# Attention into a gated FFN: a planner that knows four matmul forms, other weight and load times, and wider score steps for the fourth batch

## The chip, the cores and the metric

The kernel runs on one core of a Trainium2 chip. The metric is device time in microseconds (us) of one execution. The engines are TensorE (PE in the profile; PEld is its weight load), VectorE (DVE), ScalarE (ACT), GpSimd (POOL) and SyncE (SP), which here only issues DMAs. The clock granted to TensorE was 1.000 of full speed in the profiled execution.

## What is computed

There are 8 batches (B), 8 heads (H) and 576 rows (S) of 64 values (D). Each head sees 16 beacon keys in front of its 576 keys; the beacons are always visible, the others causally.

```
scores = q @ concat(beacon_k, k).T / sqrt(64)      # causal over k, beacons free
a      = softmax(scores)
x      = a @ concat(beacon_v, v)                   # -> 4608 rows of 512 (heads side by side)
out    = (relu(x @ w_gate) * (x @ w_val)) @ w_out  # 512 -> 1536 -> 512
```

Inputs and output are float32; the kernel multiplies in bf16 and sums in float32.

## The kernel before

**Attention.** For a batch, each of q and k comes in by pairs of heads (`load_pair`, and `load_half` for batch 0) and a rest (`load_rest`: the "K" and "Q" loads), v in five blocks (`load_v`). A load goes by SP into one of eight staging tiles `st`, is rounded to bf16 by POOL (batch 0: POOL or DVE; line 514, v line 467), turned by four products with the identity (line 525) and copied out by ACT or DVE into `kT` and `qT`. The order inside a batch is "K Q 0 0 1 1 v v 2 2 3 3 v v v v", numbered from 0.

`quad` computes the scores of two pairs of heads (a group; two groups per batch) in steps. A step (`quad_scores`, line 743) is a run of 64x64 products into PSUM banks. Each score tile then goes through `softmax`: the minimum with the mask on DVE (line 691), the exponential on ACT (line 698), the reciprocal on DVE (line 704), the scaling on POOL (line 709). `STEPS` takes few banks in a step, `STEPS2` four; which of them a batch uses is set by BIGSTEP. `last` computes the last 16 rows of all heads (line 793, 128x32 products).

`finish` turns the probabilities: on PE for batch 0 and the last rows of batches 0 and 1 (line 819), otherwise by a transposing DMA on SP (line 829, `pTb<-pb`). Then come the values: AB and CDE for each pair (line 839, 128x64 products) and F for the last rows (line 862, 128x128 products). They are copied into `xT`, the FFN's input.

**FFN.** `ffn` works on spans of rows: 240 and 336 (batch 0), then 512 each, at the end 448. For each of 12 blocks of 128 hidden columns it makes four gate products (line 900) and four value products (line 905); ACT takes the relu (line 911), DVE multiplies (line 916). Then the output products (line 931) follow, DVE or ACT copies out (lines 465 and 463), and SP stores. The weights come by nine DMAs that POOL issues and that cast on the way (line 477): gate and value for hidden columns 0, 512 and 1024, then three pieces of the output weights.

**The order.** Nothing is ordered by the program's text. Each piece of work is a `Task` with an engine, a modelled cost, dependencies, buffers it holds, and a priority; `Plan.order` simulates the engines and writes out one fixed order for each. It takes, over all engines, the task that can begin first; among equals the one with the smaller `late`, then the smaller priority number. For PE `late` is worked out from `part`, the form of the products: -1 for a task of the small form that runs now, and 1 for a task of another form that has waited less than its `lazy` time (LAZY, 20 us, for values of batches from 2 on; LAZY1, 0, for batch 1). A change of form is modelled as 0.1 us (SWITCH). Before, form 1 stands for the last rows' scores and all values (AB, CDE and F), form 2 for the score steps, form 0 for the rest.

When PE has a planned gap before 160 us, the plan puts in filler products (line 990) that compute nothing. Weights may be issued from W0 on, one in W_STEP; the score steps of batch b and group g from PACE x (b + g/2); batch 0's two parts (AB, CDE) from the times in AFTER. HELD and BEHIND name loads (batch, number) that wait: HELD until a weight piece has been issued, BEHIND until the probabilities of a group (batch, group) are scaled. The wait holds for all later loads of that batch too. It is a tiny POOL memset (line 535), on which the loads depend.

PSUM has eight banks: seven are shared from the start (at most 5 for scores, 3 for the FFN, 3 for values and turns); the eighth is the fillers' and joins at 36 us of the plan's time.

Of the kernel before, what the change touches and what calls it, by code (L numbers as in the profile page):

```python
# [17 lines left out]


BACKLOG = 4.0  # L20
RANK1 = -10.0
AHEAD = 2.0
WWORK = -15.0
FILLED = 160.0
# [5 lines left out]
LAGS = {"PE": 0.22, "ACT": 0.16, "DVE": 0.14, "POOL": 0.1, "DMA": 0.1}  # L30
LAZY = 20.0
LAZY1 = 0.0
ON_PE = 2
BIGSTEP = 3
PEQ = lambda b, g: b < 1
ENG = [("POOL", "DVE"), ("POOL",), ("POOL",)]
F_MOST = 3
HELD = {(1, 3): ('v', 0, 0), (1, 5): ('g', 0, 512), (1, 11): ('o', 0, 0)}
BEHIND = {(2, 7): (1, 1)}
MARK = 0.08  # L40
AB_FIRST = 0
W_FIRST = 0
# [4 lines left out]
ORDER0 = ("k00", "q00", "K", "Q", "k10", "q10", "v", "v", "k01", "q01", "k11", "q11", "v", "v", "v")  # L47
W_COLS = [(0, 512), (512, 512), (1024, 512)]
W_ROWS = 4
W0 = 16.5  # L50
W_STEP = 3.4
W_ISSUE = 0.85
W_MOVE = 0.72
V_MOVE = 1.25
# [3 lines left out]
FIRST_SPANS = [240, 336]  # L58
LAST_SPAN = 448
FIRST_MOST = 3  # L60
AFTER = [[0.0, 8.0]]
PACE = 39.0


class Slots:
# [104 lines left out]
class Plan:  # L170
# [7 lines left out]
    def add(self, engines, cost, run, deps=(), holds=(), prio=0.0, lag=None, part=0, lazy=0.0, after=0.0, move=0.0):  # L178
        t = Task(engines if isinstance(engines, tuple) else (engines,), cost, run, deps, holds, prio, lag, part, lazy, move)
        t.ready = after  # L180
        for d in t.deps:
            d.users.append(t)
        self.tasks.append(t)
        return t

    def order(self):
# [11 lines left out]
        part = 0  # L198
# [23 lines left out]
        while True:  # L222
            best = None
            for e in queue:
                for t in queue[e]:
                    times = begin(t, e)
                    if times is None:
                        continue
                    at, could = times
                    late = 0  # L230
                    if e == "PE":
                        late = -1 if part and t.part == part else 1 if part != t.part and at < t.ready + t.lazy else 0
                    key = (at, late, t.prio)
                    if best is None or key < best[0]:
                        best = (key, t, e)
            if best is None:
                break
            (at, _, _), t, e = best
            for x in t.engines:
                queue[x].remove(t)  # L240
            for h in t.holds:
                if h.tile is None:
                    if h.next is not None:
                        h.tile, h.next.tile = h.slots.take_pair()
                    else:
                        h.tile = h.slots.take()
            if e == "PE" and FILL_FROM < at < self.filled:
                since, tile = max(free[e], FILL_FROM), self.filler
                if at >= FILL_BANK:
                    first = min(self.banks.free, key=lambda f: f[:2], default=(at, 0, None))  # L250
                    since, tile = max(since, first[0]), first[2]
                n = int((at - since) * FILL / (0.11 if at > FILL_COLD else 0.22))
                if n > 0 and tile is not None:
                    done.append(Filler(n, tile, self.fill))
            t.start, t.engine = at, e
            cost = t.cost
            if e == "DMA":
                issue, move = cost
                if issue > 1.2:
                    wire = max(wire, at + 0.3) + move  # L260
                    free[e] = max(at + issue, wire - 0.2)
                else:
                    free[e] = at + issue
                    wire = max(wire, at + issue) + move
                end = max(wire, free[e]) + LAND
            else:
                if isinstance(cost, dict):
                    cost = cost[e]
                if e == "PE":
                    cost += SWITCH * (t.part != part)  # L270
                    part = t.part
                free[e] = end = at + cost
                if t.move:
                    wire = max(wire, end) + t.move
                    end = wire + LAND
            for h in t.holds:
                h.users -= 1
                if h.users == 0:
                    h.slots.give(end + (0.1 if e == "DMA" else LAGS[e] if t.lag is None else t.lag), h.tile)
            done.append(t)  # L280
            for u, then in [(u, end) for u in t.users] + [(u, free[e]) for u in t.soon]:
                u.ready = max(u.ready, then + (LAGS[e] if t.lag is None else t.lag))
                u.left -= 1
                if u.left == 0:
                    for x in u.engines:
                        queue[x].append(u)
# [6 lines left out]
def kernel(  # L293
# [20 lines left out]
    SK = Nb + S  # L314
# [399 lines left out]
    def quad_scores(t, g, step, phs, vals, prio, after):  # L714

        ks = (0, 1)
        if isinstance(step, tuple):
            step, ks = step[0], step[1:]

        sc = first_sc if t.b == 0 else sc_s  # L720
        banks = [[Hold(sc, 0) for _ in step] if k in ks else [] for k in range(2)]
        cols, tiles = [], []
        for b_, names in enumerate(step):
            off = 0
            for x in names:
                if x in ("E", "e"):
                    if x == "E":
                        for pair in [banks[k] for k in ks]:
                            pair[b_].next, pair[b_ + 1].prev = pair[b_ + 1], pair[b_]
                        tiles.append((512 + 64, (b_, b_ + 1), 0, mask, P * BLOCK_E))  # L730
                    lo, n, j = (0, 512, TILES) if x == "E" else (512, 64, TILES)
                else:
                    lo, n, j = 0, 64 * (x + 1), x
                    tiles.append((n, (b_,), off, mask[:, 512 + 64 - n:], P * (BLOCK if vals != ("AB",) else BLOCK_AB)[x]))
                cols.append((j, lo, n, b_, off))
                off += n

        def scores(_):
            for j, lo, n, b_, off in cols:
                for i in range(2):  # L740
                    for k in ks:
                        r = slice(64 * k, 64 * k + 64)
                        nc.tensor.matmul(banks[k][b_].tile[64 * i:64 * i + 64, off:off + n],  # L743
                                         t.q.tile[r, 2 * g + i, 64 * j:64 * j + 64],
                                         t.kT.tile[r, 2 * g + i, lo:lo + n], start=True, stop=True)

        need = [(2 * g,), (2 * g + 1,)] if t.b else [(g, 0)] if vals == ("AB",) else [(g, 0), (g, 1)]
        deps = [x for i in [*need, ("rest",)] for kind in "kq" for x in t.rows[kind, *i]]
        for x in banks[0] + banks[1]:
            x.users += 1  # L750
        s = add("PE", sum(x[2] for x in cols) / 2400.0 + 0.03, scores, deps, (*banks[0], *banks[1], *[phs[k] for k in ks], t.kT, t.q), prio, None,
                part=2, after=after)
        parts = [[], []]
        for k in ks:
            phs[k].users += 1
            for n, held, off, msk, a in tiles:
                held = tuple(banks[k][x] for x in held)
                for x in held:
                    x.users += 2
                parts[k].append((n, held, off, msk, n, on_mask, a, s))  # L760
        return parts
# [22 lines left out]
    def last(t, prio):  # L784

        ph = Hold(p_s[0], 1)
        sc = [Hold(first_sc if t.b == 0 else sc_s, 4) for _ in range(2)]
        sc[0].next, sc[1].prev = sc[1], sc[0]
        deps = [x for key, made in t.rows.items() if key[0] in "kq" for x in made]
        def scores(_):  # L790
            for bank, a, n in ((sc[0], 0, 512), (sc[1], 512, SK - 512)):
                for pp in range(NP):
                    nc.tensor.matmul(bank.tile[32 * pp:32 * pp + 32, :n], t.q.tile[:, pp, S + Nb - TAIL:],
                                     t.kT.tile[:, pp, a:a + n], start=True, stop=True)

        s = add("PE", SK / 2400.0 + 0.05, scores, deps, (*sc, ph, t.kT, t.q), prio, None, part=1)
        parts = [(SK, tuple(sc), 0, mask_f, SK - 512, on_mask_f, 0, s)]
        outs = softmax(t, parts, ph, prio, 0)
        ph.users += 1 + len(outs)
        finish(t, 0, ("F",), ph, pT_s[0], NC, [list(range(NC))] if t.b < ON_PE else [], outs, prio)  # L800

    def finish(t, p, vals, ph, pt_s, blocks, on_pe, outs, prio):
# [30 lines left out]
        def one(what):  # L833
# [8 lines left out]
            def values(_):  # L842
# [15 lines left out]
                else:  # L858
                    for pp in range(NP):
# [6 lines left out]
            nv = 2 if what == "AB" else NC  # L866
            pe = {"AB": 0.17, "CDE": 0.54, "F": 0.45}[what]
            va = add("PE", pe, values, tr + [t.rows["v", c] for c in range(nv)], (pt, ps, t.v), prio - 5, None,
                     part=1, lazy=LAZY if t.b > 1 else LAZY1 * t.b)

            def to_x(x):
                pv = ps.tile
# [151 lines left out]
```

## Time and profile before

| | |
|---|---|
| median of 3 runs | 404.94 us (404.52 to 405.55) |
| the profiled execution | 405.02 us, of which the span from the first to the last instruction is 403.3 us |
| PE busy | 388.6 us, 96% of the span |
| DVE, ACT, POOL busy | 294.8, 260.3 and 233.9 us (73%, 65%, 58%) |
| fillers (line 990) | 94 matmuls, 16.9 us busy |
| score products (line 743) | 640, 34.8 us busy |
| values (line 839) | 488, 25.7 us busy |
| FFN products (lines 905, 900, 931) | 106.3, 105.2 and 98.8 us busy |
| data moved | 67.83 MB in 173476 packets |

Busy times of PE count each matmul from its start to its modelled end, and matmuls overlap: consecutive 128x512 products start closer together than one lasts. The time something takes on PE is therefore read from start to start in the timeline, not from the mean of one instruction. The idle time in brackets behind a row is that of its engine just before it, with what ended it. In the chain of waits a row is the time from its start to the next piece of the chain.

### The profile page before, as it was taken

To read this page: it belongs to the slowest core of one execution; us is meant where nothing else is said; L and a number is where in the kernel's file an instruction comes from. 1 tells how busy PE (TensorE), PEld (TensorE's weight loads), DVE (VectorE), ACT (ScalarE), POOL (GpSimd) and SP (SyncE) were. 2 spreads that over 40 slices of the span, in tenths; PEclk is the share of its full clock that TensorE was granted. 3 is DMA by queue.
4 is the path that set the end of the run, shared out by engine and by line. 5 is a ranking of instruction groups with operands and counts; after the bars stand their busy time and mean duration, and the time that the engine had idled before them with its cause. 6 is when DMAs were issued, how large, how long until landed. Compare 5 with 4: busy or idle time off the path is not lost.

```text
span 403.3 us, 9980 instructions
## 1 busy us (share of the span) xinstructions
PE 388.6 (96%) x3276; PEld 205.8 (51%) x3316; DVE 294.8 (73%) x1046; ACT 260.3 (65%) x814; POOL 233.9 (58%) x453
## 2 busy tenths in 40 slices
PE   6999999999999999999999999999999999999994
PEld 4657855545444546455545444544454454444542
DVE  3899899896989897788797969797868633333331
ACT  2998798895877687769676878496848621320310
POOL 6899979796769469586758676676443320000000
PEclk9999999999999999999999999999999999999999
DMA  7999989999999999899999969792829074002002
GB/s 186 202 239 227 242 138 228 184 213 258 211 228 217 185 207 216 183 267 252 167 195 286 216 152 238 218 221 47 164 78 192 0 138 133 0 0 98 8 2 92
DMA packets 173476, 67.83 MB, mean 168 GB/s; under 512 B 145712, under 2 KB 168880, under 8 KB 173424
## 3 DMA queue, kind: packets, MB, share of 16 engines
q1 hardware_dynamic: 168592, 62.41, 72.7%
q0 software_dynamic: 4752, 4.72, 7.2%
q8 instruction: 26, 0.43, 0.4%
q14 instruction: 26, 0.21, 0.2%
q10 hardware_dynamic: 80, 0.07, 0.1%
HBM read 38.54 MB, written 9.44 MB: 119 GB/s over the span
## 4 chain that ended last, share of the span: by engine, by line
PE 85%; DMA 6%; POOL 3%; DVE 2%; ACT 1%; issue 1%; SPq 1%; DVEq 0%
PE f L931 23%; PE f L905 22%; PE f L900 21%; PE f L839 6%; PE f L743 6%; PE f L525 4%; DMA wv_r<-in_moe_w_val_dram 2%; DMA pTb<-pb 2%; POOL pb L709 1%; DMA st<-in_q_dram 1%; PE f L819 1%; ACT xT L698 1%; PE f L862 1%; PE f L990 1%; DVE f L691 1%
## 5 line engine op out<-in xcount | busy, mean ns | idle before, releaser
L709 POOL TENSOR_SCALAR pb<-pb,small 128x384 bf16<-128x384 bf16 (+8 forms) x272 | 141.5, 539 | 74.1 <-DVE small L704 73.4
L698 ACT ACTIVATE pb<-f,small 128x448 bf16<-128x448 f32 (+8 forms) x272 | 143.9, 554 | 27.4 <-DVE small L691 23.9
L691 DVE CUSTOM_DVE_ANT_0 f<-f,mask 128x576 f32<-128x576 f32 (+8 forms) x288 | 134.3, 513 | 13.6 <-PE f L743 9.6
L905 PE MATMUL f<-xT,wv_r 128*128 128x512 bf16 (+3 forms) x466 | 106.3, 358 | 2.3 <-DMA wv_r<-in_moe_w_val_dram 1.0
L900 PE MATMUL f<-xT,wg_r 128*128 128x512 bf16 (+3 forms) x471 | 105.2, 358 | 0.7 <-DMA wg_r<-in_moe_w_gate_dram 0.4
L916 DVE TENSOR_TENSOR hT<-g,f 128x512 bf16<-128x512 f32 (+3 forms) x120 | 75.1, 632 | 38.0 <-PE f L905 35.1
L911 ACT ACTIVATE g<-f 128x512 f32<-128x512 f32 (+3 forms) x120 | 67.0, 564 | 55.0 <-PE f L900 50.7
L931 PE MATMUL f<-wo_r,hT 128*128 128x512 bf16 (+3 forms) x439 | 98.8, 374 | 1.6 <-issue 1.1
L900 PEld LDWEIGHTS <-wg_r 128*128 128x128 bf16 x480 | 45.1, 98 | 44.3 <-issue 1.5
L905 PEld LDWEIGHTS <-wv_r 128*128 128x128 bf16 x480 | 43.8, 98 | 44.5 <-issue 5.1
L931 PEld LDWEIGHTS <-hT 128*128 128x128 bf16 (+2 forms) x456 | 41.9, 100 | 46.9 <-issue 2.9
L698 ACT ACTIVATION_READ_ACCUMULATOR pb<-f,small 128x1 f32 x272 | 60.8, 224 | 0.0
L514 POOL TENSOR_SCALAR h<-st 128x512 bf16<-128x512 f32 (+1 forms) x93 | 49.1, 542 | 12.1 <-DMA st<-in_k_dram 4.0
L691 DVE DVE_READ_ACCUMULATOR2_ANT small<- 128x1 f32 x296 | 41.9, 142 | 0.1
L465 DVE COPY osb<-f 128x512 f32<-128x512 f32 (+3 forms) x32 | 21.9, 683 | 26.1 <-PE f L931 25.9
L743 PE MATMUL f<-kT,qT 64*64 64x512 bf16 (+7 forms) x640 | 34.8, 295 | 0.1
L525 PE MATMUL f<-ident,h 128*128 128x128 bf16 (+1 forms) x320 | 28.1, 221 | 1.4 <-POOL h L514 1.2
L704 DVE RECIPROCAL small<-small 128x1 f32<-128x1 f32 (+3 forms) x144 | 22.0, 161 | 8.9 <-ACT pb L698 6.4
L525 PEld LDWEIGHTS <-h 128*128 128x128 bf16 (+1 forms) x320 | 21.3, 100 | 14.0 <-POOL h L514 3.2
L743 PEld LDWEIGHTS <-qT 64*64 64x64 bf16 x640 | 14.4, 106 | 23.1 <-issue 18.6
L839 PE MATMUL f<-pTb,v 128*64 128x320 bf16 (+3 forms) x488 | 25.7, 253 | 0.5 <-DMA pTb<-pb 0.5
L839 PEld LDWEIGHTS <-v 128*64 128x64 bf16 (+1 forms) x512 | 20.9, 109 | 8.9 <-issue 4.5
(61 smaller groups left out, 233.8 us busy)
## 6 DMA issues: line engine op xcount, KB each, us to landing
out_dram<-osb SPq DMA_DIRECT2D x34, 256.0 KB, 2.5
st<-in_k_dram SPq DMA_DIRECT2D x32, 256.0 KB, 4.1
st<-in_q_dram SPq DMA_DIRECT2D x32, 256.0 KB, 4.5
st<-in_v_dram SPq DMA_DIRECT2D x24, 256.0 KB, 5.8
st<-in_v_dram SPq DMA_DIRECT2D x8, 224.0 KB, 4.9
wg_r<-in_moe_w_gate_dram POOLq DMA_DIRECT2D x3, 512.0 KB, 7.4
wv_r<-in_moe_w_val_dram POOLq DMA_DIRECT2D x3, 512.0 KB, 7.6
wo_r<-in_moe_w_out_dram POOLq DMA_DIRECT2D x3, 512.0 KB, 7.6
```

Source lines behind the costliest of these rows:

```text
L514: (nc.gpsimd if x.engine == "POOL" else nc.vector).tensor_scalar(to, src, by, 1.0, ALU.mult, ALU.mult)
L525: nc.tensor.matmul(to, h16.tile[:rows, a * P:(a + 1) * P], ident[:rows, :rows], start=True, stop=True)
L691: nc.vector.tensor_tensor_reduce(out=view(i, n - m), in0=view(i, n - m), in1=msk, scale=1.0, scalar=at(7) if m < n else 3.0e38, op0=ALU.ad ...
L698: nc.scalar.activation(ph.tile.rearrange("p a n -> p (a n)")[:, a:a + n], view(i), AF.Exp, bias=at(i), scale=-1.0, accum_out=at(4 + i))
L709: nc.gpsimd.tensor_scalar(one, one, at(8 + i), 1.0, ALU.mult, ALU.mult)
L743: nc.tensor.matmul(banks[k][b_].tile[64 * i:64 * i + 64, off:off + n], t.q.tile[r, 2 * g + i, 64 * j:64 * j + 64], t.kT.tile[r, 2 * g + i, ...
L839: nc.tensor.matmul(ps.tile[64 * hh:64 * hh + 64, d0:d0 + w], t.v.tile[:rows, c, D * h:D * h + D], rhs(64 * hh), start=(c == 0), stop=(c == ...
L900: nc.tensor.matmul(psg.tile[:, :mt], wg_r[:, ki, nf * P:(nf + 1) * P], xT[:, ki, m0:m0 + mt], start=(ki == 0), stop=(ki == KM - 1))
L905: nc.tensor.matmul(psv.tile[:, :mt], wv_r[:, ki, nf * P:(nf + 1) * P], xT[:, ki, m0:m0 + mt], start=(ki == 0), stop=(ki == KM - 1))
L911: r = add("ACT", c_act(mt), lambda _, psg=psg, g=g: nc.scalar.activation(g.tile[:, :mt], psg.tile[:, :mt], AF.Relu), (a,), (psg, g), -1000 ...
L916: hid.append(add("DVE", c_dve(mt), lambda _, psv=psv, g=g, nf=nf: nc.vector.tensor_mul(hT[nf].tile[:, :mt], g.tile[:, :mt], psv.tile[:, :m ...
L931: nc.tensor.matmul(ps[c].tile[64 * c:64 * c + rows, :w], hT[nf].tile[:, t0:t0 + rows], wo_r[:, nf, w * c:w * c + w], start=(nf == 0), stop ...
```

## The change

- **Forms.** F values become form 0 (they are 128x128 products like the FFN's), the last rows' scores form 3. So form 1 is AB and CDE, 2 the score steps, 3 the last rows' scores. A task of a small form gets `late` = NEXT = -0.5 when another small form is running, whether its `lazy` time is over or not. `SLAZY` gives score steps of batches from 2 on a lazy time of 0.0, which is what they had.
- **Steps.** BIGSTEP goes from 3 to 2: batch 3 uses `STEPS2`, as batches 4 to 7 do.
- **Weights and loads.** W0 goes from 16.5 to 14.0 and W_STEP from 3.4 to 1.4. HELD: all of batch 1's loads wait until the first value piece is issued, from number 2 (pair 0) until the third gate piece is, from number 4 (pair 1) until the third value piece is. Before, numbers 3, 5 and 11 waited for the first value piece, the second gate piece and the first output piece. RANK1, the priority of batch 1's loads, goes from -10 to -14.
- **Batch 2.** Its loads from number 2 (pair 0) wait for batch 1's first group; as before, from number 7 they wait for its second.
- **Starts.** Batch 0's CDE scores may begin at 12 and not 8; PACE goes from 39 to 38.

```diff
-RANK1 = -10.0
+RANK1 = -14.0
...
+SLAZY = 0.0
+NEXT = -0.5
 ON_PE = 2
-BIGSTEP = 3
+BIGSTEP = 2
...
-HELD = {(1, 3): ('v', 0, 0), (1, 5): ('g', 0, 512), (1, 11): ('o', 0, 0)}
-BEHIND = {(2, 7): (1, 1)}
+HELD = {(1, 0): ("v", 0, 0), (1, 2): ("g", 0, 1024), (1, 4): ("v", 0, 1024)}
+BEHIND = {(2, 2): (1, 0), (2, 7): (1, 1)}
...
-W0 = 16.5
-W_STEP = 3.4
+W0 = 14.0
+W_STEP = 1.4
...
-AFTER = [[0.0, 8.0]]
-PACE = 39.0
+AFTER = [[0.0, 12.0]]
+PACE = 38.0
...
                     if e == "PE":
-                        late = -1 if part and t.part == part else 1 if part != t.part and at < t.ready + t.lazy else 0
+                        late = -1 if part and t.part == part else NEXT if part and t.part else 1 if part != t.part and at < t.ready + t.lazy else 0
...
         s = add("PE", sum(x[2] for x in cols) / 2400.0 + 0.03, scores, deps, (*banks[0], *banks[1], *[phs[k] for k in ks], t.kT, t.q), prio, None,
-                part=2, after=after)
+                part=2, after=after, lazy=SLAZY if t.b > 1 else 0.0)
...
-        s = add("PE", SK / 2400.0 + 0.05, scores, deps, (*sc, ph, t.kT, t.q), prio, None, part=1)
+        s = add("PE", SK / 2400.0 + 0.05, scores, deps, (*sc, ph, t.kT, t.q), prio, None, part=3)
...
             va = add("PE", pe, values, tr + [t.rows["v", c] for c in range(nv)], (pt, ps, t.v), prio - 5, None,
-                     part=1, lazy=LAZY if t.b > 1 else LAZY1 * t.b)
+                     part=0 if what == "F" else 1, lazy=LAZY if t.b > 1 else LAZY1 * t.b)
```

## The prediction

> **What bounds the kernel.** I read the page's busy line first.
>
> ```profile
> PE 388.6 (96%) x3276; PEld 205.8 (51%) x3316; DVE 294.8 (73%) x1046; ACT 260.3 (65%) x814; POOL 233.9 (58%) x453
> ```
>
> TensorE is busy for 96% of the span, and the change takes no product away; only what is not product can go: filler matmuls, idle time, and changes of form. Next come windows: PE as a whole, then the same with line 990 (the fillers) alone. Columns are start:end, length, busy time with the number of instructions, granted clock, DMA share and GB/s; the second view has PEld behind PE.
>
> ```profile
> 10.00:20.00 10.00, 9.72 (x117) 1.00 1.01 204
> 20.00:26.50 6.50, 6.25 (x73) 1.00 1.18 222
> 26.50:40.00 13.50, 12.17 (x144) 1.00 1.22 237
> 40.00:390.00 350.00, 346.04 (x2850) 1.00 0.80 167
> ```
> ```profile
> 10.00:20.00 10.00, 5.99 (x42) 3.72 (x43) 1.00 1.01 204
> 20.00:26.50 6.50, 3.66 (x23) 1.79 (x23) 1.00 1.18 222
> 26.50:40.00 13.50, 1.93 (x10) 0.81 (x10) 1.00 1.22 237
> ```
>
> Between 40 and 390 us PE idles 350 - 346.04 = 4.0 us. The waste is early, and the timeline shows what ends it:
>
> ```profile
> 20.79 0.94 PE L990 MATMUL f<-mask,ident 128*128 128x256 bf16 x7
> ...
> 26.54 0.99 PE L900 MATMUL f<-xT,wg_r 128*128 128x240 bf16 x8
> 28.14 0.99 PE L905 MATMUL f<-xT,wv_r 128*128 128x240 bf16 x8 [0.61 <-DMA wv_r<-in_moe_w_val_dram]
> ...
> 34.06 0.58 PE L900 MATMUL f<-xT,wg_r 128*128 128x240 bf16 x4 [0.38 <-DMA wg_r<-in_moe_w_gate_dram]
> ...
> 37.41 0.58 PE L905 MATMUL f<-xT,wv_r 128*128 128x240 bf16 x4 [0.35 <-DMA wv_r<-in_moe_w_val_dram]
> ```
>
> Seven fillers take 0.94 us, some 0.11 us each once they overlap (the last one's tail, about 0.2, left off). From 26.5 to 40 that is 10 x 0.11 = 1.1 us, plus 13.5 - 12.17 = 1.3 us idle: 2.4 us in which PE has rows ready and waits for weights. Before 26.5 it is 65 fillers, 7.1 us, but there the first span's rows (all heads' AB values of batch 0) do not exist yet.
>
> The second narrow place is the end of batch 1. Timelines of SP, POOL and PE, and the window there with all engines (PE, PEld, DVE, ACT, POOL):
>
> ```profile
> 60.42 0.38 SPq L554 DMA_DIRECT2D st<-in_k_dram  x1
> ...
> 64.55 10.89 SPq L829 DMA_TRANSPOSE pTb<-pb  x2
> ...
> 79.37 9.11 SPq L829 DMA_TRANSPOSE pTb<-pb  x2
> ```
> ```profile
> 68.06 0.62 POOL L514 TENSOR_SCALAR h<-st 128x512 bf16<-128x512 f32 x1 [0.43 <-PE f L525]
> ...
> 78.14 1.20 POOL L709 TENSOR_SCALAR pb<-pb,small 128x576 bf16<-128x576 bf16 x2 [2.42 <-DVE small L704]
> ```
> ```profile
> 64.56 0.31 PE L525 MATMUL f<-ident,h 80*128 80x80 bf16 x4
> ...
> 79.25 0.41 PE L743 MATMUL f<-kT,qT 64*64 64x64 bf16 x8
> ...
> 87.94 0.88 PE L839 MATMUL f<-pTb,v 128*64 128x128 bf16 x16 [0.46 <-DMA pTb<-pb]
> ...
> 92.40 0.88 PE L839 MATMUL f<-pTb,v 128*64 128x128 bf16 x16
> ...
> 94.11 1.03 PE L900 MATMUL f<-xT,wg_r 128*128 128x512 bf16 x3
> ```
> ```profile
> 80.00:90.00 10.00, 9.44 (x106) 4.86 (x109) 9.40 (x46) 9.25 (x35) 9.61 (x23) 1.00 1.22 209
> ```
>
> The third span, 512 rows of batch 1, starts at 94.11, right behind batch 1's last values. Those hang on the transposes issued at 79.37, and these on a norm at 78.14 that had waited 2.42 us for DVE. PE meanwhile uses up batch 0's products: at 87.94 it waits. So whatever is saved before 40 us is only kept if batch 1 ends earlier too; otherwise the idle time moves to about 85 us.
>
> **Part 1: weights earlier, batch 1's loads behind them** (W0, W_STEP, HELD, AFTER, RANK1).
>
> ```profile
> 17.20 0.93 POOL L477 DMA_DIRECT2D wg_r<-in_moe_w_gate_dram  x1
> ...
> 28.04 0.79 POOL L477 DMA_DIRECT2D wv_r<-in_moe_w_val_dram  x1
> ...
> 36.61 0.79 POOL L477 DMA_DIRECT2D wv_r<-in_moe_w_val_dram  x1
> ```
> ```profile
> DMA to landing us min/median/max: 6.9/7.6/9.3
> ```
> ```profile
> 18.90 0.38 SPq L554 DMA_DIRECT2D st<-in_k_dram  x1
> ...
> 41.86 1.78 POOL L514 TENSOR_SCALAR h<-st 128x512 bf16<-128x512 f32 x3
> ...
> 47.96 0.63 PE L743 MATMUL f<-kT,qT 64*64 64x64 bf16 x16
> ```
>
> The six gate and value pieces go out from 17.20 to 36.61, one in 3.9 us. With W0 14 the first may leave some 3 us earlier (POOL runs batch 0's norms at 14, so not more), and as batch 1's loads stand behind them the gap shrinks towards 3.3 us. That puts the sixth at 14.2 + 5 x 3.3 = 31, and each landing 3 to 5 us earlier: the three waits of 0.61, 0.38 and 0.35 and the ten fillers go, up to 2.4 us. The three output pieces follow them and lie beside the products. What is moved back: batch 1's first pairs, issued from 18.90, now wait for the fifth and sixth piece (27 to 31 us), about 9 us later. That costs nothing while POOL casts those tiles only at 41.86, behind batch 0's norms; the first scores of batch 1 stand at 47.96. With 7 us from issue to landing, as a weight takes, the cover is 41.9 - 31 - 7 = 4 us. SP takes its queue in order, but behind the waiting loads stand only more loads; its first transpose is the one at 64.55. AFTER 12 holds batch 0's CDE scores 4 us longer, which leaves DVE and ACT to the AB part; nothing in the trace prices it, so I bound it at 1 us either way and take zero. RANK1 only reorders loads against weights that have -15 and batch 0 that has -20; it stays between them: zero.
>
> The DMA share in the windows of 20 to 40 us is already 1.18 to 1.22 with weights and loads in flight together. The Trainium skill (DMA: Bandwidth & Descriptors, section Issuing engines are not separate DMA queues) says that DMAs started by the scalar, sync or gpsimd engine share the same 16 DMA engines and interleave. By that rule an earlier issue alone buys no earlier landing, only the removal of other traffic does; the landings from 6.9 to 9.3 us agree. With it alone the gain would be 0, a rival below.
>
> **Part 2: batch 2's pairs wait for batch 1's first group; PACE 38** (BEHIND). Batch 2's pairs were issued from 60.42, their casts and transposes (64.56, 68.06) and evictions ran in batch 1's softmax. Now they stand behind the group whose transposes occupy SP from 64.55 to 75.44. Queued behind on SP are batch 2's remaining loads and no one else's work. That takes five tiles off POOL (5 x 0.62 = 3.1 us) and their evictions off DVE and ACT before the norm at 78.14, and PACE lets batch 1's second group begin at 57 and not 58.5. I estimate batch 1's end 2.5 us earlier, between 0 (the chain is latency) and 5. But PE also loses fillers of real work before 90 us: batch 2's transposes from 64.56 and its scores from 79.25 come later, about 1 to 2 us of PE work. For the later groups PACE moves work in a stage where PE never starves: zero.
>
> Parts 1 and 2 together give the smaller of 2.4 (weights) and 2.5 (batch 1's end), less half a microsecond for the displaced batch 2 work: -2.0 us. Bounds: -3.4, with 1 us more from AB, and +4.5, the fourth rival's case.
>
> **Part 3: forms.**
>
> ```profile
> 139.44 1.89 PE L900 MATMUL f<-xT,wg_r 128*128 128x512 bf16 x8
> 141.17 1.03 PE L905 MATMUL f<-xT,wv_r 128*128 128x512 bf16 x4
> 142.12 0.41 PE L743 MATMUL f<-kT,qT 64*64 64x192 bf16 x8
> ```
> ```profile
> 217.22 0.81 PE f L839 x16
> ...
> 291.82 1.50 PE f L839 x32
> ```
> ```profile
> 18.93 0.36 PE L839 MATMUL f<-xT,v 128*64 128x128 bf16 x6
> ...
> 337.45 1.57 PE L839 MATMUL f<-pTb,v 128*64 128x128 bf16 x32
> ```
>
> Eight products take 141.17 - 139.44 = 1.73 us, four 0.865; the four before a score step take 142.12 - 141.17 = 0.95. So entering a small form costs 0.09 us. Leaving costs 2 x 0.81 - 1.50 = 0.12 (two trips of 16 against one of 32). A trip of values or of the last rows' scores (lines 839, 793) that stands directly behind or before a score step saves one change, 0.1 us. In the PE timeline 22 such trips stand without a score step beside them, the first at 18.93, the last at 337.45; two come behind the last scores and three in batch 0's gap without scores, so 17 can go: 1.7 us. NEXT also ends the patience of 20 us at the first score step, so a group's two pairs, which land 4 to 6 us apart, may go behind two steps instead of as one trip of 32: one change more in perhaps half of 12 groups, 0.6 back, less where they were split already. I take -1.3, between -2.0 and -0.3. F as form 0 is what its 128x128 tiles are; its products then need no company: zero.
>
> Values that go out sooner can wait for their transpose on PE. Batch 1, whose patience was zero before (LAZY1), shows that: one wait in four trips, the 0.46 above, 0.12 on average. For 24 pairs 2.8 us is the bad end, 0 the good one; behind a score step there are some 2 us of cover on average (steps are about 5 apart), so I take +0.4.
>
> **Part 4: batch 3 in steps of four banks** (BIGSTEP).
>
> ```profile
> 119.37 0.63 PE L743 MATMUL f<-kT,qT 64*64 64x64 bf16 x16
> ...
> 129.21 0.56 PE L743 MATMUL f<-kT,qT 64*64 64x512 bf16 x12
> ```
>
> Batch 3's first group makes four trips in the PE timeline, these two the first and the last; STEPS2 makes three. Two groups: 2 x 0.21 = -0.4 us. Eight reciprocals less are DVE time beside PE's. Four banks must be free at once; batch 4's groups do it already. Bounds -0.5 and +0.6.
>
> **Sum:** -2.0 - 1.3 + 0.4 - 0.4 = -3.3 us against the profiled run's 405.02 (span 403.3 and 1.7 around it; 0.1 above the median 404.94): **401.7 us**. Less than 0.3% (1.2 us) can hardly be told from no change.
>
> **Rivals.** (a) More gain: the AB part is 1 us faster too, all 17 trips merge, no value waits: 405.0 - 3.4 - 1.7 - 0.4 = 399.5. For: DVE and POOL are what AB waits for; against: POOL still issues weights in the midst of it. (b) Only the forms pay: weights are issued earlier but land no earlier, or batch 1's end stays at 90.5 and PE waits there: 405.0 - 1.3 - 0.4 + 0.4 = 403.7, and 0.5 to 1 more for batch 2's displaced work, about 404.3. For: the full DMA share and the chain of SP's two transposes, 9.11 us, which no part shortens. (c) Slower: the sixth weight leaves POOL not at 31 but near 36 (the old gap of 3.9 from a start at 16.5), so batch 1's pairs land behind 41.9; every microsecond past that shifts 47.96 and 92.40 alike, and PE has no other work left at 85 us. Four late, half a microsecond of displaced work and the forms' gain: 405.0 + 4.0 + 0.5 - 1.3 = 408 us. It decides if the pairs land after 42 us. Against it: 4 us of cover.
>
> **Chances:** forecast (400.3 to 403.6) 0.49, (a) 0.15, (b) 0.15, (c) 0.21. Faster by over 0.3% 0.64, within 0.3% 0.15, slower 0.21. The likeliest case's own range is 400.3 to 403.6; for 8 in 10 the range reaches into (a) and part of (c): 398.8 to 407.0.
>
> **What would show it.** Line 990 with far fewer than ten matmuls after 26.5 us; no PE waits for wg_r and wv_r; the first batch 1 scores near 47; the transposes of 79.37 at about 77 and the third span before 92; values right behind line 743 in the PE timeline; three score trips per group from 115 to 150. Wrong would be: PE idle between 80 and 92 of over 2 us, waits on pTb in many places, or a first batch 1 score after 49.

## The result and the profile after

| | before | changed |
|---|---|---|
| median of 13 runs each | 404.38 us (403.36 to 406.24) | 401.90 us (400.57 to 405.01) |
| the profiled execution, its span | 405.02 us, 403.3 us | 402.93 us, 401.1 us |
| instructions of ACT | 814 | 826 |

The ratio is 0.9942 with a 95% interval of 0.9919 to 0.9964: 2.5 us less, between 1.5 and 3.3. The predicted 401.7 us is met to 0.2 us; the predicted gain was 3.3 us, from a first profile of 405.02. The traces say that most of the gain came from a place that the prediction does not mention.

First the views that the prediction read, for the changed kernel. Line numbers are two higher than before (the fillers are line 992, the gate products 902, the values 841). The busy line, then PE by windows, then the fillers alone (columns as in the prediction):

```profile
PE 389.5 (97%) x3267; PEld 205.4 (51%) x3310; DVE 288.8 (72%) x1026; ACT 264.1 (66%) x826; POOL 234.9 (59%) x454
```
```profile
10.00:20.00 10.00, 9.90 (x108) 1.00 1.27 234
20.00:26.50 6.50, 5.78 (x68) 1.00 1.20 197
26.50:40.00 13.50, 13.35 (x160) 1.00 1.15 212
40.00:390.00 350.00, 345.94 (x2837) 1.00 0.80 167
```
```profile
10.00:20.00 10.00, 6.51 (x42) 4.05 (x42) 1.00 1.27 234
20.00:26.50 6.50, 3.44 (x22) 1.72 (x21) 1.00 1.20 197
26.50:40.00 13.50, 0.88 (x5) 0.36 (x5) 1.00 1.15 212
```

From 26.5 to 40 us PE is now busy 13.35 us and not 12.17, with 5 fillers and not 10: the waits for weights are gone. But from 20 to 26.5 it is busy 5.78 and not 6.25, and the fillers are about as many as before (22 and 23). From 40 to 390 us the idle time is 4.1 us (4.0 before). Most of that is not idle time: both profiles lack some 40 matmul records (3276 where PEld has 3316 weight loads, 3267 where it has 3310). In a second profile of each, shown below, no record is missing, and the same window has 0.3 us idle before and 1.0 changed. The timeline of PE, cut to the points that the prediction named:

```profile
23.74 0.73 PE L821 MATMUL f<-ident,xT 128*128 128x128 bf16 x8 [0.72 <-POOL xT L711]
...
26.57 0.99 PE L902 MATMUL f<-xT,wg_r 128*128 128x240 bf16 x8
...
47.96 0.63 PE L745 MATMUL f<-kT,qT 64*64 64x64 bf16 x16
...
89.70 0.88 PE L841 MATMUL f<-pTb,v 128*64 128x128 bf16 x16
...
91.97 1.04 PE L902 MATMUL f<-xT,wg_r 128*128 128x512 bf16 x3
```

The first span begins at 26.57 (26.54 before), batch 1's first scores stand at 47.96 as before, and the third span begins at 91.97, 2.1 us earlier. SP and POOL show why: batch 1's first pair is issued at 30.52, batch 1's second transposes at 76.55 (79.37 before), and the sixth weight piece leaves POOL at 31.67.

```profile
30.52 0.39 SPq L556 DMA_DIRECT2D st<-in_k_dram  x1
...
76.55 9.58 SPq L831 DMA_TRANSPOSE pTb<-pb  x2
```
```profile
14.97 0.94 POOL L479 DMA_DIRECT2D wg_r<-in_moe_w_gate_dram  x1
...
22.37 0.79 POOL L479 DMA_DIRECT2D wg_r<-in_moe_w_gate_dram  x1
23.20 0.93 POOL L711 TENSOR_SCALAR xT<-xT,small 128x256 bf16<-128x256 bf16 x2
...
31.67 0.79 POOL L479 DMA_DIRECT2D wv_r<-in_moe_w_val_dram  x1
...
41.96 1.19 POOL L516 TENSOR_SCALAR h<-st 128x512 bf16<-128x512 f32 x2
```

Now the end of both timelines, which the prediction's windows (up to 390 us) left out: the kernel before, then the changed one.

```profile
397.64 0.37 ACT L463 COPY osb<-f 64x256 f32<-64x256 f32 x1 [9.44 <-PE f L931]
398.04 2.41 ACTq L945 DMA_DIRECT2D out_dram<-osb  x1
```
```profile
397.53 0.37 ACT L465 COPY osb<-f 64x256 f32<-64x256 f32 x1 [9.44 <-PE f L933]
397.92 0.58 ACTq L947 DMA_DIRECT2D out_dram<-osb  x1
```

The last copy follows the last product. It begins at 397.64 and at 397.53 us: at that point the two kernels are 0.1 us apart. Then ACT issues the last store, which takes 2.41 us before and 0.58 us after; its data land at 401.89 and 400.02. (SP issues the other part of this store; its data land at 400.06 and 400.20, so the last landing is at 401.89 and 400.20.) Of the 2.2 us between the two spans, 0.1 stand before the last copy and 1.6 between it and the last landing. The other 0.5 lie behind the last landing, where the span goes on for 1.42 us before and 0.91 changed.

### The profile page after: what moved, and what is told of

Same layout as the page of the kernel before. It is cut to its first block, busy times and chain, and to the rows that moved or that the text cites. A ratio compares the mean times of both kernels' runs of the same rounds, so it can differ in the third digit from the quotient of the medians.

```text
span 401.1 us, 9952 instructions
## 1 busy us (share of the span) xinstructions
PE 389.5 (97%) x3267; PEld 205.4 (51%) x3310; DVE 288.8 (72%) x1026; ACT 264.1 (66%) x826; POOL 234.9 (59%) x454
## 4 chain that ended last, share of the span: by engine, by line
PE 82%; POOL 6%; DMA 3%; DVE 2%; issue 2%; SPq 2%; ACT 2%; ACTq 0%; POOLq 0%; DVEq 0%
PE f L933 24%; PE f L907 20%; PE f L902 20%; PE f L745 6%; PE f L841 5%; PE f L527 4%; POOL pb L711 2%; DMA st<-in_k_dram 2%; POOL xT L711 2%; POOL h L516 1%; DVE f L693 1%; DMA st<-in_beacon_k_dram 1%; PE f L864 1%; PE f L821 1%; ACT pb L700 1%
## 5 line engine op out<-in xcount | busy, mean ns | idle before, releaser
L711 POOL TENSOR_SCALAR pb<-pb,small 128x576 bf16<-128x576 bf16 (+8 forms) x272 | 142.2, 543 | 69.2 <-DVE small L706 68.6
L700 ACT ACTIVATE pb<-f,small 128x448 bf16<-128x448 f32 (+8 forms) x272 | 144.1, 554 | 25.8 <-DVE small L693 18.5
L907 PE MATMUL f<-xT,wv_r 128*128 128x512 bf16 (+3 forms) x463 | 107.4, 358 | 0.9
L933 PE MATMUL f<-wo_r,hT 128*128 128x512 bf16 (+3 forms) x439 | 100.1, 374 | 1.2 <-issue 0.5
L465 ACT CAST xT<-f 128x240 bf16<-128x240 f32 (+2 forms) x58 | 21.5, 378 | 28.1 <-PE f L841 25.8
L467 DVE COPY osb<-f 128x512 f32<-128x512 f32 (+2 forms) x31 | 21.1, 682 | 26.2 <-PE f L933 24.3
L527 PE MATMUL f<-ident,h 128*128 128x128 bf16 (+1 forms) x320 | 29.8, 222 | 2.5 <-POOL h L516 1.9
L706 DVE RECIPROCAL small<-small 128x2 f32<-128x2 f32 (+3 forms) x136 | 20.8, 161 | 14.8 <-ACT pb L700 10.1
L841 PE MATMUL f<-pTb,v 128*64 128x320 bf16 (+3 forms) x488 | 26.7, 253 | 0.1
L469 POOL TENSOR_SCALAR v<-st 128x512 bf16<-128x512 f32 (+1 forms) x38 | 23.2, 621 | 4.1 <-DMA st<-in_v_dram 4.1
```

The source lines that it names most:

```text
L527: nc.tensor.matmul(to, h16.tile[:rows, a * P:(a + 1) * P], ident[:rows, :rows], start=True, stop=True)
L700: nc.scalar.activation(ph.tile.rearrange("p a n -> p (a n)")[:, a:a + n], view(i), AF.Exp, bias=at(i), scale=-1.0, accum_out=at(4 + i))
L711: nc.gpsimd.tensor_scalar(one, one, at(8 + i), 1.0, ALU.mult, ALU.mult)
L841: nc.tensor.matmul(ps.tile[64 * hh:64 * hh + 64, d0:d0 + w], t.v.tile[:rows, c, D * h:D * h + D], rhs(64 * hh), start=(c == 0), stop=(c == ...
L907: nc.tensor.matmul(psv.tile[:, :mt], wv_r[:, ki, nf * P:(nf + 1) * P], xT[:, ki, m0:m0 + mt], start=(ki == 0), stop=(ki == KM - 1))
L933: nc.tensor.matmul(ps[c].tile[64 * c:64 * c + rows, :w], hT[nf].tile[:, t0:t0 + rows], wo_r[:, nf, w * c:w * c + w], start=(nf == 0), stop ...
```

## The experiments

**The same two kernels again.** One profile each could mislead, so both ran once more.

> The kernel before once more, unchanged, for a second profile. In its first profile the last DMA issue on ACT (the 64-row half of the last store) took 2.41 us and landed at 401.89, where the changed kernel's took 0.58 and landed at 400.02, while the last product ended at 397.57 and 397.46. If that belongs to the program (it has 505 instruction rows on ACT against 523), it is there again: ACT issue over 2 us and some 2 us of the gain lie behind the last product. If it was one execution's, the issue takes 0.58, the last product ends 2 us later than in the changed kernel, at 399 to 400, and the gain lies in PE's order as I predicted.

> The changed kernel once more, unchanged, beside the kernel before on the same chip, for a second profile: last product at 396 to 398, ACT issue 0.58, 0.994 of before.

Before: 404.59 us against 405.23 for the runs beside it, 0.999 (0.9977 to 1.0003). Changed: 402.22, 0.9931 (0.9909 to 0.9953). The end of the kernel before, then of the changed one:

```profile
396.68 0.37 ACT L463 COPY osb<-f 64x256 f32<-64x256 f32 x1 [9.44 <-PE f L931]
397.07 2.50 ACTq L945 DMA_DIRECT2D out_dram<-osb  x1
```
```profile
397.27 0.37 ACT L465 COPY osb<-f 64x256 f32<-64x256 f32 x1 [9.46 <-PE f L933]
397.67 0.58 ACTq L947 DMA_DIRECT2D out_dram<-osb  x1
```

In this pair the changed kernel's PE is done 0.6 us later, and its execution is still 1.4 us shorter (402.74 against 404.15). The long issue comes back, and so does the difference behind the last landing (1.42 us before, 0.96 changed).

These two profiles also give an account of PE. For each product I took the time to the next product's start and subtracted what its columns take at full clock (512 columns in 216 ns, the prediction's 1.73 us for eight), shared where two or four small tiles run side by side. Fillers count as lost as a whole. What is left is lost time, in us:

```
from        0    10   26.5    40    95   140   340 | sum    useful
before    7.26 11.42  4.89  7.81  4.31 13.93  0.76 | 50.38  344.0
changed   6.98 12.35  4.11  8.23  4.10 14.43  0.77 | 50.97  344.0
```

0.8 us are won between 26.5 and 40 us, and 0.9 are lost between 10 and 26.5. Up to 95 us the sums are 31.4 and 31.7: the third span begins earlier, but PE has not lost less. From 95 to 340 us, where the forms and batch 3's steps were to pay, the sums are 18.2 and 18.5. The windows of PE agree (before, then changed): 1.0 us more is busy from 26.5 to 40 us, 1.3 less just before, and from 40 to 95 no time is idle in either.

```profile
20.00:26.50 6.50, 6.34 (x73) 1.00 1.18 228
26.50:40.00 13.50, 12.43 (x147) 1.00 1.22 233
40.00:95.00 55.00, 55.00 (x590) 1.00 1.04 209
```
```profile
20.00:26.50 6.50, 5.09 (x58) 1.00 1.25 221
26.50:40.00 13.50, 13.44 (x164) 1.00 1.16 217
40.00:95.00 55.00, 54.99 (x586) 1.00 0.99 211
```
 
POOL shows what took the 0.9 (before, then changed):

```profile
20.41 0.79 POOL L477 DMA_DIRECT2D wv_r<-in_moe_w_val_dram  x1
...
21.69 1.32 POOL L709 TENSOR_SCALAR xT<-xT,small 128x192 bf16<-128x192 bf16 x3
22.99 1.03 POOL L709 TENSOR_SCALAR pb<-pb,small 128x320 bf16<-128x320 bf16 x2
...
25.29 0.79 POOL L477 DMA_DIRECT2D wg_r<-in_moe_w_gate_dram  x1
```
```profile
18.56 0.79 POOL L479 DMA_DIRECT2D wv_r<-in_moe_w_val_dram  x1
...
22.34 0.79 POOL L479 DMA_DIRECT2D wg_r<-in_moe_w_gate_dram  x1
23.18 0.93 POOL L711 TENSOR_SCALAR xT<-xT,small 128x256 bf16<-128x256 bf16 x2
```

Before, the AB norms (`xT`) end at 23.0 and the third weight is issued behind them, at 25.29. Changed, it is issued at 22.34 in front of the last two norms, which end at 24.1. PE's turn of these rows then waits 0.75 us for POOL (0.72 in the row at 23.74 above; 0.2 before), and in this pair the first span begins 1.1 us later (before, then changed):

```profile
26.41 0.99 PE L900 MATMUL f<-xT,wg_r 128*128 128x240 bf16 x8
```
```profile
27.54 0.99 PE L902 MATMUL f<-xT,wg_r 128*128 128x240 bf16 x8
```

In the first pair it began at the same time (26.54 and 26.57).

**Is the end a matter of the change?** ACT runs 814 instructions before and 826 after. Sixteen one-element copies at ACT's start shift all that follows and leave PE's order alone.

```diff
+    pads = many(2, [1, 1], FP32, "pad")
+    nc.vector.memset(pads[0], 0.0)
+    for _ in range(16):
+        nc.scalar.copy(pads[1], pads[0])
     for t in plan.order():
```

> The kernel before with 16 copies of one element on ACT ahead of everything else; the plan and the order on PE, SP and the other engines are the same. In both profiles of before ACT fetches 8192 bytes of instructions 0.6 us after its last DMA issue begins, and that issue takes 2.4 to 2.5 us. My new theory, that this fetch and not PE's order makes most of the difference to the changed kernel: the fetch falls earlier, where ACT has time, the issue takes 0.58, the last product ends as before and the time is 1.9 us less, 0.995 of before. The old one, that the gain lies in PE's order: 1.000 of before, no more than 0.3 us for the tail.

403.06 us against 405.28 for the kernel before, 0.9957 (0.9928 to 0.9986): with PE's old order, 2.2 us less by the medians and 1.7 by the ratio. The issue is short:

```profile
402.38 0.58 ACTq L945 DMA_DIRECT2D out_dram<-osb  x1
```

(This profiled execution, 407.78 us, has PE at half clock for 3.4 us from 30.0, so only its end and its DMA records are read.) Behind the last landing the span goes on for 1.41 us, as in the kernel before. The trace's DMA records name the likely cause of the long issue. Queue 14, of the kind "instruction", moves packets of 8192 bytes:

```
                       ACT's last issue   took   queue 14 packets nearest it
before                      398.04        2.41   398.6, 403.6
before again                397.07        2.50   397.7, 402.7
before, ACT shifted         402.38        0.58   381.6, 406.3
forms alone                 399.45        0.57   375.1
changed                     397.92        0.58   374.2
changed again               397.67        0.58   374.1
```

Only where such a packet starts 0.6 us behind the beginning of the issue is the issue long. In the eight profiles of other kernels that are not in this table the issue takes 0.57 to 0.58 us, and no such packet starts within 3 us of it. That the place in ACT's program decides is shown by the shift. The records don't name the engine that a packet serves, but the shift tells it: the shifted execution ends 4.3 us later (last copy at 401.99), and most late packets of 8192 bytes move with it (311.9 us before, 316.2 shifted; 334.0 and 338.4). Some stand earlier all the same (222.4 and 216.9; 298.5 and 296.3), and the one at the end most of all (398.6 and 381.6). ACT's program is the one that had grown, by 16 instructions and DVE's by one. That such a packet is ACT's next block of instructions, and that the issue waits for it, is inferred.

**The parts alone.** Forms and NEXT put into the kernel before:

```diff
+NEXT = -0.5
-late = -1 if part and t.part == part else 1 if ...
+late = -1 if part and t.part == part else NEXT if part and t.part else 1 if ...
-... prio, None, part=1)
+... prio, None, part=3)
-                     part=1, lazy=LAZY if t.b > 1 else LAZY1 * t.b)
+                     part=0 if what == "F" else 1, lazy=LAZY if t.b > 1 else LAZY1 * t.b)
```

> The kernel before with the forms alone (F values form 0, last rows' scores form 3, NEXT). My theory, the merged trips: 1.3 us faster, 0.997 of before. The rival, that the planner only exchanges one kind of trip for another (its PE order has 190 changes of form against 188): the same within 0.5 us.

405.02 against 405.08 us: 1.0000 (0.9971 to 1.0029). Its end is short (0.57, in the table above), but ACT's last issue begins at 399.45 and not at 398.04 (397.07 in the second profile of before): PE is at least 1.4 us later, and the end gives that back. The order that comes out has 190 changes of form against 188.

The weights alone, in the kernel before:

```diff
-HELD = {(1, 3): ('v', 0, 0), (1, 5): ('g', 0, 512), (1, 11): ('o', 0, 0)}
+HELD = {(1, 0): ("v", 0, 0), (1, 2): ("g", 0, 1024), (1, 4): ("v", 0, 1024)}
-W0 = 16.5
-W_STEP = 3.4
+W0 = 14.0
+W_STEP = 1.4
```

> The kernel before with W0 14, W_STEP 1.4 and the new HELD alone; batch 2 does not wait. My theory says the saved time moves to the end of batch 1: PE waits near 85 us and the time is the same within 0.5 us. Rival one, that the early gain is kept anyway: 1.7 us faster. Rival two, that the parts only pay together because the planner's order is rewritten as a whole (its PE order has 112 fillers and 205 changes of form against 94 and 188): 18 x 0.11 + 17 x 0.1 = 3.7 us slower.

409.81 us, 1.0108 (1.0070 to 1.0146): slower. PE's timeline at batch 1's end:

```profile
96.47 1.36 PE L990 MATMUL f<-mask,ident 128*128 128x256 bf16 x11
97.76 0.88 PE L839 MATMUL f<-pTb,v 128*64 128x128 bf16 x16
...
99.14 1.89 PE L900 MATMUL f<-xT,wg_r 128*128 128x512 bf16 x8
```

PE has nothing to do but fillers before batch 1's last values, and the third span begins at 99.14, 5 us later than before. In this execution (411.04 us) PE also ran 3.4 us at half clock from 25.4. The other four had a granted clock of 1.000 and took 409.3 to 410.3 us, so the half clock is not what makes this kernel slower.

The other three leave one part out of the changed kernel. Batch 2 as before:

```diff
-BEHIND = {(2, 2): (1, 0), (2, 7): (1, 1)}
+BEHIND = {(2, 7): (1, 1)}
```

> The changed kernel without the new wait of batch 2's pairs. My theory: batch 1's last values come up to 2.5 us later, 1.5 to 2.5 us slower than the changed kernel, and PE or its fillers show it between 70 and 95 us. The rival, that the wait is not needed for the early gain: the same within 0.7 us as the changed kernel.

409.31 us, 1.0103 (1.0052 to 1.0154) against the kernel before, 1.6% above the changed one. PE's timeline and the clock (windows of all engines):

```profile
140.43 2.03 PE L992 MATMUL f<-mask,ident 128*128 128x256 bf16 x17
143.42 0.88 PE L841 MATMUL f<-pTb,v 128*64 128x128 bf16 x16 [0.96 <-DMA pTb<-pb]
```
```profile
26.50:40.00 13.50, 13.22 (x130) 8.96 (x130) 10.50 (x44) 10.79 (x32) 10.83 (x21) 0.78 1.07 190
```

PE runs dry at batch 2's end and not at batch 1's, and it runs at half clock for 6.8 us from 25.6. Here the clock counts: three executions with a granted clock of 1.000 took 407.2 to 408.6 us, three with 0.992 to 0.994 took 410.0 to 412.7 (the profiled one 412.33). At full clock this kernel is still some 5 us slower than the changed one.

The weights, HELD and AFTER as before:

```diff
-HELD = {(1, 0): ("v", 0, 0), (1, 2): ("g", 0, 1024), (1, 4): ("v", 0, 1024)}
+HELD = {(1, 3): ('v', 0, 0), (1, 5): ('g', 0, 512), (1, 11): ('o', 0, 0)}
-W0 = 14.0
-W_STEP = 1.4
+W0 = 16.5
+W_STEP = 3.4
-AFTER = [[0.0, 12.0]]
+AFTER = [[0.0, 8.0]]
```

> The changed kernel with W0 16.5, W_STEP 3.4, the HELD and the AFTER of before. My theory: the waits for weights between 26 and 40 us are back and with them 2 us of the gain, so 0.999 of before or so. The rival, that the forms and steps carry the gain: it stays within 0.7 us of the changed kernel, 0.994 of before.

407.19 us, 1.0035 (1.0009 to 1.0061). This is 0.9% above the changed kernel, and a wait of PE for weights is back (engine, line, what it waited for, us, times, longest):

```profile
PE f L907 <- DMA wv_r<-in_moe_w_val_dram: 1.9, 1, 1.9
```

The wait of 1.9 us is about half of the difference of 3.8. The other half fits 16 fillers (2.1 us busy) that run behind 100 us, where the changed kernel has none.

The forms without NEXT:

```diff
-late = -1 if part and t.part == part else NEXT if part and t.part else 1 if ...
+late = -1 if part and t.part == part else 1 if ...
```

> The changed kernel with the four forms but without NEXT. My theory, the merged trips: up to 1.3 us slower than the changed kernel. The rival, that what NEXT does is to let values go when they are ready, not to save changes: the planner's PE order has 138 fillers against 88 and 188 changes against 186, so 50 x 0.11 = 5 us slower, with the loss where the fillers stand and not spread over the score steps.

412.77 us, 1.0196 (1.0157 to 1.0235). PE's timeline:

```profile
90.08 3.88 PE L992 MATMUL f<-mask,ident 128*128 128x256 bf16 x34
93.89 0.88 PE L841 MATMUL f<-pTb,v 128*64 128x128 bf16 x16
...
95.25 1.89 PE L902 MATMUL f<-xT,wg_r 128*128 128x512 bf16 x8
```

Here is the place that the prediction's first part warns of: PE has used up everything at 90 us, and 34 fillers run until batch 1's values land. Another 16 follow at batch 2's end (142 to 146 us).

**The price of a change of form.** In the last span a 64x64 product with 64 columns goes ahead of each block's gate and value products; the control has a full 128x128 product with the same columns. They write banks that are overwritten at once, so the output is untouched.

```diff
+                if m0 + mt == NT:
+                    nc.tensor.matmul(psg.tile[:64, :64], ident[:64, :64], mask.bitcast(BF16)[:64, :64], start=True, stop=True)
...
+                if m0 + mt == NT:
+                    nc.tensor.matmul(psv.tile[:64, :64], ident[:64, :64], mask.bitcast(BF16)[:64, :64], start=True, stop=True)
```

> The changed kernel, and in the last span (gate and value products only, PE never waits) a tiny 64x64 product of 64 columns in front of each of the 24 gate and value blocks, into the bank that the block then overwrites: 24 trips to a small form more and nothing else. My price, 0.09 us in and 0.12 us out, gives 24 x 0.21 = 5.0 us more than the changed kernel, less than 1 us of it for the products. The rival, that a change of form costs little beside the pipeline: under 2 us.

> The control for the small trips: the same 24 tiny products of 64 columns in the 128x128 form, so no change of form. Both theories: 24 x 0.03 = 0.7 us more than the changed kernel. The difference between the two kernels is the price of 48 changes of form.

408.59 and 402.85 us: 5.7 us for 24 trips, 0.24 for one, 0.12 for a change. (Values and last rows' scores have other forms, 128x64 and 128x32, which were not priced.) The timeline of the small form, then of the control:

```profile
372.49 0.93 PE L904 MATMUL f<-xT,wg_r 128*128 128x448 bf16 x4
373.35 0.21 PE L909 MATMUL f<-mask,ident 64*64 64x64 bf16 x1
373.50 0.93 PE L911 MATMUL f<-xT,wv_r 128*128 128x448 bf16 x4
```
```profile
372.67 0.92 PE L911 MATMUL f<-xT,wv_r 128*128 128x448 bf16 x4
373.43 0.19 PE L909 MATMUL f<-mask,ident 128*128 128x64 bf16 x1
373.45 0.92 PE L911 MATMUL f<-xT,wv_r 128*128 128x448 bf16 x4
```

One round takes 1.01 us (373.50 less 372.49) against 0.78. The Trainium skill (TensorEngine Tiling (Array Packing), Key Properties) says that changing the tiling mode drains TensorE; the rows fit that, and about 0.1 us is what a change costs here.

**Steps of two banks for batch 3.**

```diff
-BIGSTEP = 2
+BIGSTEP = 3
```

> The changed kernel with BIGSTEP 3, batch 3 in steps of two banks as before. My theory: 0.4 us slower than the changed kernel, about 0.995 of before. The rival, by the planner's PE order (197 changes of form against 186, 88 fillers in both): 1.1 us slower. Another, that DVE's eight reciprocals (1.3 us) count in a stage where DVE is 85% busy: over 2 us slower.

403.38 us, 0.9964 (0.9943 to 0.9984), where the changed kernel has 0.9931 to 0.9942: about 1 us in favour of four banks, with intervals that overlap. The planned order has 197 changes of form and not 186; at 0.12 us the 11 would be 1.3 us, so the run fits the price of the changes as well as that of the steps.

**Fewer changes of form.** The values of batches from 2 on are held 6 us before NEXT applies, so that two pairs go as one trip again, and the last rows' scores wait up to 6 us for company.

```diff
-late = -1 if part and t.part == part else NEXT if part and t.part else 1 if ...
+late = -1 if part and t.part == part else NEXT if part and t.part and at >= t.ready + (0.0 if t.part != 1 or t.lazy == 0.0 else 6.0) else 1 if ...
-... prio, None, part=3)
+... prio, None, part=3, lazy=6.0 if t.b > 1 else 0.0)
```

> The changed kernel, with values of batches from 2 on held 6 us before NEXT counts for them, so that a group's two pairs go together more often, and the last rows' scores allowed to wait 6 us for a small form. The planner's PE order has 178 changes of form against 186 and 89 fillers against 88. At the measured price of 0.12 us a change: 1.0 us faster than the changed kernel, about 0.991 of before. The rival, that the softmax and transposes behind a later value step undo it: the same within 0.5 us or slower.

178 changes of form against 186, 403.40 us, 0.9952 (0.9923 to 0.9981). The 8 x 0.12 = 1.0 us are not seen beside the changed kernel's 0.9931 to 0.9942; the intervals are too wide to exclude a part of them.

## Why the prediction was right, and where not

**The sum.** 401.7 was forecast and 401.9 measured, but by other terms: the number was met by luck. It also helped that the gain of 3.3 was taken from 405.02, where the median of 13 runs is 404.38. In the first pair of profiles 2.1 of the 2.2 us lie behind the start of the last copy, 1.6 with the long issue and 0.5 behind the last landing. The sum has neither: it starts from "the profiled run's 405.02 (span 403.3 and 1.7 around it; 0.1 above the median 404.94)" without asking what fills the 5.7 us of the span behind the start of the last copy (403.3 less 397.64). PE's own order, to which all of the -3.3 was put, gained 0.1 us in the first pair of profiles and lost 0.6 in the second. In the ratios 0.6 to 1.1 us lie between the shifted kernel before (0.9957) and the changed one (0.9931 to 0.9942). About 0.5 of that is the part behind the last landing, which the shift left as it was; 0.1 to 0.6 us are left for PE's order, and the intervals don't tell that from zero.

**Weights earlier, up to 2.4 us.** The mechanism held: sixth piece at 31.67 (predicted 31), no wait of PE for `wg_r` or `wv_r`, 5 fillers after 26.5 in place of 10. (In the second pair it is 11 against 10, as six fillers at 26.52 stand in front of the late first span.) What it brought to PE was 0.8 us in that pair, and 0.9 went on POOL. The step that failed is "Before 26.5 it is 65 fillers, 7.1 us, but there the first span's rows (all heads' AB values of batch 0) do not exist yet", taken as untouched: the issues take 0.8 to 1.1 us of POOL's time each, three of them instead of two now stand ahead of the norms that make these rows, and the prediction counted that only as an argument against rival (a). AFTER and RANK1 were taken at zero, and rightly: with either at its old value the planner writes the same order on every engine.

**Batch 1's end 2.5 us earlier.** Transposes at 76.55 (77 predicted), third span at 91.97 (before 92). The step that failed is the sentence behind it, "Parts 1 and 2 together give the smaller of 2.4 (weights) and 2.5 (batch 1's end)". PE has next to no idle time before that point in either kernel: in the second pair all 55 us from 40 to 95 are busy in both, and lost time up to 95 us is nearly equal. Starting a span earlier on a full PE moves batch 2's transposes and scores behind it, and saves nothing. The 4.0 us of idle time that the prediction read between 40 and 390 us are for the most part missing records. PACE was not changed alone.

**The warning was right, and larger.** "Whatever is saved before 40 us is only kept if batch 1 ends earlier too; otherwise the idle time moves": weights alone (1.1% above the kernel before) and no NEXT (2.0%) show it at 90 to 99 us. Without BEHIND it appears at batch 2's end, a place that the prediction did not look at.

**Forms, -1.3 us.** The price was right for the score form: 0.21 a trip predicted, 0.24 measured. The count failed: "17 can go". The order has 186 changes of form where it had 188. Values do go behind score steps now, but often as two trips of 16 in place of one of 32, and 9 trips of values and 7 of the last rows' scores still stand alone. The term is -0.2 us by this price, and PE's lost time from 95 to 340 us did not fall at all. The stalls of +0.4 on `pTb` did not come: no row of PE's waits names it.

**Batch 3's steps, -0.4 us.** Three trips per group, as said; the run with two banks, about 1 us slower, agrees in sign and is too close to give a size or to tell steps from changes of form.

**The rivals.** (a) needed the AB part to be faster; in the second pair it ended 1.1 us later. (c) did not happen: the first pair of batch 1 is issued at 30.52 and POOL still casts at 41.96, the first scores stand at 47.96. (b), in which only the forms pay, had the right doubt about the first parts, but the forms didn't pay either; its other reason, the full DMA share, held no weight back: the share is still 1.15 to 1.27 from 10 to 40 us, and no wait for weights is left. A rival was missing: PE's order is worth next to nothing, and the end decides.

What stays open: how much of the 2.5 us is PE's, between 0 and about 0.6 us; what shortens the span behind the last landing by 0.5 us; and how the long issue waits for the packet.

## What to carry to other kernels

Before a difference of half a per cent is put to an order of work, read the last rows of both timelines: an issue of 2.4 us where others take 0.6 is a fixed toll that a change in the number of instructions may remove. An earlier start of a stage is a saving only if the busy engine had been idle for it; count lost time up to that point in both traces. Parts of a planned order don't add up: leaving out any of three parts here costs 0.9 to 2.6%, while all of them together win little or nothing over the order before them.

## What the runs showed of the hardware

- A DMA issue on ACT that coincides with an 8192-byte packet of the instruction queue took 2.41 and 2.50 us in place of 0.57 to 0.58; sixteen instructions more in front of it removed that.
- A change between 128x128 products and a 64x64 product cost 0.12 us; by the rows of the two kernels 0.10 going in (0.86 against 0.76 for four products) and 0.13 going out (0.15 against 0.02).
- PE fell to half clock for one stretch of 3.4 us (weights alone, ACT shifted) or 6.8 us (batch 2 not behind) between 25.4 and 33.4 us, with products and fillers running and single gaps of 0.2 to 2.7 us in front. The Trainium skill (TensorE: Matmul & The Clock Gate, Part 1) gives windows of 3413 ns and an idle window of about 3.4 us as what brings the half clock; the lengths agree, the condition does not, since no gap was that long. Nor does PE's busy share over that length decide: in the 3.41 us right before the fall PE was busy for 0.96 us (ACT shifted), 1.30 (weights alone) and 2.18 (batch 2 not behind), while the kernel with the weights as before was busy for 1.80 of the 3.42 us from 26.19 and stayed at full clock.
